# Attention stage cut into nine units instead of eleven, with fractional stage offsets, integer phases, and dense down products two parts behind

## The chip, the cores and the metric

The kernel runs on one core of a Trainium2 chip. The metric is the time of one execution on the device in microseconds (us). TensorE (PE in the profile) multiplies matrices, and its weight loads have a row of their own (PEld); VectorE is DVE, ScalarE is ACT, GpSimd is POOL, and SyncE (SP) issues most of the transfers.

## What is computed

Three layers in a row, in float32: a linear attention with a complex decay, a mixture of experts with one expert for each token, and a dense gated layer.

```python
# attention: batch 4, 8 heads, 768 tokens, head width 48
mag = np.sqrt(a_re * a_re + a_im * a_im)
scale = np.minimum(mag, 0.999) / (mag + 1e-06)
a_re_n, a_im_n = (a_re * scale, a_im * scale)
for t in range(S):
    ar, ai = (a_re_n[:, :, t, :, None], a_im_n[:, :, t, :, None])
    new_re = ar * S_re - ai * S_im
    new_im = ar * S_im + ai * S_re
    kv = np.einsum('bhd,bhe->bhde', k[:, :, t], v[:, :, t])
    S_re, S_im = (new_re + kv, new_im)
    y[:, :, t] = np.einsum('bhd,bhde->bhe', q[:, :, t], S_re)
# experts: 3072 tokens of width 384, 8 experts with 1024 hidden
logits = x @ w_gate + modality_bias[modality_id]
e_idx = np.argmax(logits, axis=1)             # gate_w: softmax value of that expert
out[mask] = gate_w[mask, None] * (np.maximum(x[mask] @ w1[e], 0.0) @ w2[e])
# dense: hidden 1536
g = x @ w_gate
silu = g * (1.0 / (1.0 + np.exp(-g)))
return (silu * (x @ w_val)) @ w_out
```

## The kernel before

**Attention.** The recurrence is worked in 24 chunks, one for each batch b and each stretch t of 128 tokens, all 8 heads at once. A chunk is a tile of 128 tokens by 384 (8 heads x 48). The decays become logarithms and angles. A product with a triangular matrix (`tri`) sums them along the tokens; the decay's sum is exponentiated into p and r = 1/p, the angle's sum is the phase, and sine and cosine of the phase stand in `tr`. k·r and q·p times `tr` give K and Q of 768 columns a chunk (L597). PE transposes them, multiplies them (L656), DVE masks the product with the triangle (`am`, L661), PE multiplies with v and adds the carried state (L670, L673), ACT copies the result (`yT`), and PE reorders it together with the router's logits (L684, "x of a chunk" below). L684 thus marks that a chunk of attention is done. The state (`S`) and the last phase (`carry`) go on to the chunk of the same batch at the next t.

**Units.** The elementwise stages are issued for a unit of up to three chunks, so an instruction has 384, 768 or 1152 columns. Before, `CUTS` makes eleven units of 1, 2, 3, 3, 3, 3, 3, 2, 2, 1 and 1 chunks. Chunks are counted c0 to c23 and units u0, u1, ... here. The stages of a unit are load_a (the decays a_re and a_im into `ar` and `ai`), a1 and a2 (logarithms, clamps), angle (arctangent), decay and sum (the two products with `tri` and what reads them), load_b (q, k, v), trig (sine and cosine), prod (k·r, q·p, K, Q), attend, and route (softmax, expert, position in the expert's region, rows written to DRAM by POOL).

**Who sets the order.** Each stage adds its operations to a planner (`Plan`, L24). The order in which they are added is the program's: `todo` sorts (u + lag, stage, u), with whole-number lags in `ROUND`. The planner (`order`, L79) then simulates the engines with cost estimates: at each step it emits the operation that can start earliest, a tie going to the one added first. `bias` adds a handicap to a choice of DVE and to a change of ACT's function table. Each engine runs its list strictly in the order emitted. Tiles come from rings of one to five buffers, so a new tile waits for the last reader of the old one.

**The phase before.** For each chunk ACT turns the phase in PSUM into a whole number of turns (`ki`, L533), DVE subtracts that many turns (`tw`, L538), and a clamp (L562) and an absolute value (L571, in place) run for each unit between and around the sine and the cosine.

**Experts.** The eight slots hold up to 396 rows each. The first slot's expert is guessed from the routing after unit uGU (before: GU = 5, 15 chunks), so its rows (`xg`) and weights (`st`) are fetched while attention still runs; first and second slot are planned with the attention stage. A slot is 8 hidden blocks of up products (L976), relu (`hh`, `hl`), down products (L990). Weights are split into two halves of bits: a cast (L1004, `w1h`, `w2h`) and a difference (L1006). Before the second slot's up products, every engine reads a flag `miss` (was the guess wrong?) and branches; before, that reading stands after the plan.

**Dense layer.** 8 blocks of 384 tokens and 12 parts of the hidden width: 96 rounds of 18 up products (pg, pv, L1517), the gate on ACT and DVE (L1520 to L1522, `hd` L1420 and L1421), and 9 down products (po, L1537: 3 groups t of 128 tokens, 3 products each). A round's down products follow the next round's up products. `write` (L1539) copies three groups (ACT, L1542) and POOL writes each to DRAM (L1544).

## Time and profile before

| | |
|---|---|
| median of 3 runs | 974.35 us (973.89 to 974.85) |
| the profiled execution's own time | 973.59 us |
| its span, first to last instruction | 971.8 us |
| mean granted TensorE clock | 0.984 of 2.4 GHz |
| PE, PEld busy | 913.3 us (94%), 868.8 us (89%) |
| DVE, ACT busy | 606.6 us (62%), 458.1 us (47%) |
| POOL busy | 115.6 us (12%) |
| bytes moved | 64.57 MB |

The profile times every instruction of one execution from the span's start. "Idle before" is the time that an engine stood still ahead of an instruction, and the arrow names what ended it. Attention fills about 0 to 280 us, the first slot 280 to 310 us, the other slots 311 to 501 us, and the dense layer what is left. The shares above are means over all of these.

### The profile page before, as it was taken

How to read it: one execution, taken by the hardware profiler on the slowest of the kernel's cores; microseconds unless marked ns; L12 is line 12 of the kernel's file. 1: busy time of each engine (PE TensorE's matmuls, PEld its weight loads, DVE VectorE, ACT ScalarE, POOL GpSimd, SP SyncE). 2: the span in 40 equal slices, each digit the busy share in tenths (PEclk: the TensorE clock that was granted, in tenths of full speed). 3: DMA queues.
4: the chain of work that ended last, by engine and by line, in shares of the span. 5: the costliest groups of instructions: out<-in, count | busy, mean ns of one | idle time of the engine just before them, and what ended most of it. 6: DMA issues, size and time to landing. Idle time of an engine off the chain costs nothing. (4 is left out here: it accounts for less than half of the span.)

```text
span 971.8 us, 15775 instructions
## 1 busy us (share of the span) xinstructions
PE 913.3 (94%) x5982; PEld 868.8 (89%) x5982; DVE 606.6 (62%) x1215; ACT 458.1 (47%) x798; POOL 115.6 (12%) x212
## 2 busy tenths in 40 slices
PE   2687999999988999999998899999999999999997
PEld 1466888988878999999997799999999999999996
DVE  6789989887775888788868843434333343433332
ACT  6787888786664555545444332322222232222222
POOL 2122022231220011111100010000101000010101
PEclk9887999999999999999999999999999999999999
DMA  9997365547422557333221000000000000000000
GB/s 170 161 183 142 74 132 101 101 100 206 117 65 75 95 97 215 78 78 88 55 67 49 1 25 1 1 25 1 25 1 26 1 9 17 1 25 1 25 1 25
DMA packets 155670, 64.57 MB, mean 66 GB/s; under 512 B 135564, under 2 KB 150212, under 8 KB 155588
## 3 DMA queue, kind: packets, MB, share of 16 engines
q1 hardware_dynamic: 147588, 39.82, 21.9%
q0 software_dynamic: 8000, 23.69, 9.2%
q8 instruction: 48, 0.79, 0.4%
q14 instruction: 34, 0.28, 0.1%
HBM read 67.86 MB, written 14.37 MB: 85 GB/s over the span
## 5 line engine op out<-in xcount | busy, mean ns | idle before, releaser
L1537 PE MATMUL po<-w,hd 128*128 128x384 f32 x864 | 168.9, 339 | 6.5 <-ACT hd L1420 6.4
L1517 PE MATMUL pg<-xb,w 128*128 128x384 f32 x864 | 166.1, 336 | 1.3 <-ACTq L1481 1.3
L1517 PE MATMUL pv<-xb,w 128*128 128x384 f32 x864 | 165.5, 336 | 0.0
L1537 PEld LDWEIGHTS po<-w,hd 128*128 128x128 f32 x864 | 150.4, 188 | 11.9 <-ACT hd L1420 9.1
L1521 DVE TENSOR_TENSOR sg<-sg,pg 128x384 f32<-128x384 f32 x96 | 53.2, 554 | 164.6 <-ACT sg L1520 164.6
L1517 PEld LDWEIGHTS pg<-xb,w 128*128 128x128 f32 x864 | 152.1, 188 | 1.6 <-ACTq L1481 1.6
L1517 PEld LDWEIGHTS pv<-xb,w 128*128 128x128 f32 x864 | 151.2, 188 | 0.0
L1420 ACT CAST hd<-sg 128x384 fp32r<-128x384 f32 x96 | 49.3, 513 | 161.3 <-DVE sg L1522 161.3
L1520 ACT ACTIVATE sg<-pg 128x384 f32<-128x384 f32 x96 | 47.2, 491 | 162.5 <-PE pg L1517 162.5
L1421 DVE TENSOR_TENSOR hd<-sg,hd 128x384 fp32r<-128x384 f32 x96 | 53.6, 558 | 55.6 <-ACT hd L1420 55.6
L1522 DVE TENSOR_TENSOR sg<-sg,pv 128x384 f32<-128x384 f32 x96 | 53.2, 554 | 37.3 <-PE pv L1517 36.3
L1544 POOL DMA_INDIRECT out_dram<-o,idu x24 | 23.1, 964 | 410.4 <-ACT o L1542 407.3
L976 PE MATMUL banks<-xh,w1h 128*128 128x396 f32 x192 | 67.0, 349 | 2.3 <-DVEq L1226 2.3
L979 ACT ACTIVATE hh<-banks 128x396 fp32r<-128x396 f32 x64 | 32.1, 502 | 76.0 <-PE banks L976 74.0
L976 PE MATMUL banks<-xh,w1l 128*128 128x396 f32 x192 | 66.2, 345 | 0.0
L983 DVE SCALAR_TENSOR_TENSOR hl<-banks,hh 128x396 fp32r<-128x396 f32 x64 | 36.3, 567 | 31.5 <-ACT hh L979 31.0
L656 PEld LDWEIGHTS banks<-tQ,tK 96*128 96x128 f32 x384 | 48.2, 196 | 5.2 <-issue 2.4
L656 PE MATMUL banks<-tQ,tK 96*128 96x128 f32 x384 | 52.2, 284 | 0.5 <-ACT tQ L380 0.4
L990 PE MATMUL banks<-hl,w2h 128*128 128x396 f32 x192 | 47.9, 344 | 1.2 <-DVE hl L983 1.2
L990 PE MATMUL banks<-hh,w2h 128*128 128x396 f32 x192 | 47.8, 343 | 0.3 <-ACT hh L979 0.3
L990 PE MATMUL banks<-hh,w2l 128*128 128x396 f32 x192 | 47.7, 343 | 0.0
L976 PE MATMUL banks<-xl,w1h 128*128 128x396 f32 x192 | 45.6, 346 | 0.0
(216 smaller groups left out, 1556.4 us busy)
## 6 DMA issues: line engine op xcount, KB each, us to landing
st<-in_moe_w_dram SPq DMA_DIRECT2D x64, 384.0 KB
xrows<-zero SPq DMA_DIRECT2D x8, 597.1 KB
xg<-xrows SPq DMA_DIRECT2D x8, 597.1 KB
ar<-in_a_re_dram SPq DMA_DIRECT2D x24, 192.0 KB
ai<-in_a_im_dram SPq DMA_DIRECT2D x24, 192.0 KB
q<-in_q_dram SPq DMA_DIRECT2D x24, 192.0 KB
k<-in_k_dram SPq DMA_DIRECT2D x24, 192.0 KB
v<-in_v_dram SPq DMA_DIRECT2D x24, 192.0 KB
```

What stands on the lines that cost most here:

```text
L656: pe.matmul(plan[ap][:, i * P : (i + 1) * P], plan[kt][:, i, :], plan[qt][:, i, :], start=True, stop=True)
L976: pe.matmul(ps[:, :SLOT], a[:, g, o : o + P], x[:, g, :], start=(n == 0), stop=(n == 3 * G3 - 1))
L979: sc.activation(out=hidden(s, f)[0], in_=ps[:, :SLOT], func=AF.Relu)
L983: ve.scalar_tensor_tensor(out=hl, in0=ps[:, :SLOT], scalar=0.0, in1=hh.bitcast(F32), op0=ALU.max, op1=ALU.subtract)
L990: pe.matmul(pds[:, g, :SLOT], w[:, f % 2, g * P : (g + 1) * P], x, start=(f == 0 and term == 0), stop=(f == KF1 - 1 and term == 2))
L1420: sc.copy(dst[0], src)
L1421: ve.tensor_tensor(out=dst[1], in0=src, in1=dst[0].bitcast(F32), op=ALU.subtract)
L1517: pe.matmul(p_, a[:, g, :], x[:, g, :n_], start=(n == 0), stop=(n == 3 * G3 - 1))
L1520: sc.activation(out=sg, in_=ps[0], func=AF.Sigmoid)
L1521: ve.tensor_tensor(out=sg, in0=sg, in1=ps[0], op=ALU.mult)
L1522: ve.tensor_tensor(out=sg, in0=sg, in1=ps[1], op=ALU.mult)
L1537: pe.matmul(p_[:, :DM], h[:, sl], w, start=(f == 0 and i == 0), stop=(f == KF2 - 1 and i == 2))
```

## The change

1. The attention stage has nine units: 2, 3, 3, 3, 3, 3, 2, 2 and 3 chunks.
2. Each stage's lag is a fraction of a round (`LAG`), scaled by 0.95 for the first two units, so the program's order and the planner's choices change throughout.
3. The phase: ACT writes the sum times 2^25/2π as an int32 straight into `tw`. For each unit DVE then shifts left by 7 (whole turns fall out of the word) and multiplies the int32 by π/2^31 into float32. L538 and L562 go, with the tile `ki`. The absolute value goes to a tile `ta` of its own; `jk` (a discarded output) goes to `w`. The carried phase is taken after the multiplication.
4. The guess of the first expert comes after u3 (11 chunks) instead of u5 (15 chunks).
5. Reading the flag `miss` becomes an operation inside the plan.
6. The planner's bias numbers and the estimate for the constants' load change.
7. In the dense layer a round's down products come two rounds later; at the end, the last two parts run group by group, each group written as soon as it is done.

```diff
-    CUTS = (1, 2, 3, 3, 3, 3, 3, 2, 2, 1, 1)
+    CUTS = (2, 3, 3, 3, 3, 3, 2, 2, 3)
...
+    SHL = 7
+    TURN = 2.0 ** (32 - SHL)
+    RAD = 3.1415925 / 2.0**31
...
+            def f_tw(e, c=c, pk=pk):
+
+                if e == "ACT":
+                    sc.activation(out=plan[tw][:, c, :].bitcast(I32), in_=plan[pk][:, :DM], func=AF.Copy, scale=TURN / TWO_PI)
...
+        def f_shl():
+
+            ve.tensor_scalar(out=flat(tw).bitcast(I32), in0=flat(tw).bitcast(I32), scalar1=SHL, scalar2=None,
+                             op0=ALU.logical_shift_left)
+
+        def f_rad():
+            ve.tensor_scalar(out=flat(tw), in0=flat(tw).bitcast(I32), scalar1=RAD, scalar2=None, op0=ALU.mult)
...
-            def f_tw(c=c, pk=pk, kk=kk):
-                ve.scalar_tensor_tensor(out=plan[tw][:, c, :], in0=plan[kk], scalar=-TWO_PI, in1=plan[pk][:, :DM],
-                                        op0=ALU.mult, op1=ALU.add)
...
-        def f_cl():
-            ve.tensor_scalar(out=flat(tw), in0=flat(tw), scalar1=3.1415925, scalar2=-3.1415925, op0=ALU.min, op1=ALU.max)
...
-    exv, g_row, GU = {}, [], 5
+    exv, g_row, GU = {}, [], 3
...
-    ROUND = (("load_a", 0), ("angle", 1), ("trig", 2), ("a1", 0), ("load_b", 1), ("a2", 0), ("decay", 1),
-             ("prod", 2), ("sum", 1), ("attend", 2), ("route", 3))
-    todo = sorted((u + lag, i, u, nm) for i, (nm, lag) in enumerate(ROUND) for u in range(NU))
+    LAG = dict(load_a=0.00, angle=1.30, trig=2.25, a1=1.00, load_b=2.35, a2=1.00, decay=1.45, prod=2.45, sum=1.65, attend=2.90, route=4.55)
+    todo = sorted((u + lag * (1 if u >= 2 else 0.95), i, u, nm) for i, (nm, lag) in enumerate(LAG.items()) for u in range(NU))
...
-    plan.emit(rank=lambda o, p: o["i"], delta=0, bias={'DVE': 2.0, 'table': 0.6}, pins={'sx': 'ACT', 'abs': 'DVE', 'ki': 'ACT'})
+    missing = []
+    plan.op("SP", 0.0, lambda: missing.append(nc.values_load(miss32[0:1, 0:1], min_val=0, max_val=1000001)), r=["miss"])
+    plan.emit(rank=lambda o, p: o["i"], delta=0.00, bias={'DVE': 1.41, 'table': 0.37}, pins={'sx': 'ACT', 'abs': 'DVE', 'ki': 'ACT'})
...
-    miss = nc.values_load(miss32[0:1, 0:1], min_val=0, max_val=1000001)
-    missed = tc.If(miss > 0, label="missed")
+    missed = tc.If(missing[0] > 0, label="missed")
...
-        if n > 0:
-            jp, fp = seq[n - 1]
+
+        if 1 < n < len(seq) - 1:
+            jp, fp = seq[n - 2]
             down2(jp, fp)
             if fp == KF2 - 1:
                 write(jp)
-    down2(*seq[-1])
-    write(len(BLKS) - 1)
+
+    down2(*seq[-3])
+    for t in range(BLK // P):
+        for jp, fp in seq[-2:]:
+            down2(jp, fp, (t,))
+        write(len(BLKS) - 1, (t,))
```

Line numbers of the changed kernel differ: x of a chunk is L696 there, first-slot up and down products L988 and L1002, the split's cast L1016, the dense products L1529 and L1550.

**SP at the start of the program, before.** Each row is a run of transfers of one chunk each (128x8x48) into the ring buffers of `ar`, `ai`, q, k and v; a unit's `ar` and `ai` come first, and its q, k and v later.

```order
L403 DMA ar_157<-in_a_re_dram 128x8x48
L403 DMA ai_160<-in_a_im_dram 128x8x48
L403 DMA ar_158<-in_a_re_dram 128x8x48 x2
L403 DMA ai_161<-in_a_im_dram 128x8x48 x2
L403 DMA q_168<-in_q_dram 128x8x48
L403 DMA k_170<-in_k_dram 128x8x48
L403 DMA v_172<-in_v_dram 128x8x48
L403 DMA ar_159<-in_a_re_dram 128x8x48 x3
L403 DMA ai_162<-in_a_im_dram 128x8x48 x3
L403 DMA q_169<-in_q_dram 128x8x48 x2
```

The same stretch of SP in the changed kernel:

```order
L407 DMA ar_157<-in_a_re_dram 128x8x48 x2
L407 DMA ai_160<-in_a_im_dram 128x8x48 x2
L407 DMA ar_158<-in_a_re_dram 128x8x48 x3
L407 DMA ai_161<-in_a_im_dram 128x8x48 x3
L407 DMA ar_159<-in_a_re_dram 128x8x48 x3
L407 DMA ai_162<-in_a_im_dram 128x8x48 x3
L407 DMA q_168<-in_q_dram 128x8x48 x2
L407 DMA k_170<-in_k_dram 128x8x48 x2
L509 DMA pe_206<-p_174 16x1x48 x2
L407 DMA v_172<-in_v_dram 128x8x48 x2
```

The decays of three units (8 chunks, 16 transfers) now stand ahead of the first q and k; before, three chunks' decays (6 transfers) did.

**ACT at the end of the first slot, before.** `hh` are relu rows of the first slot, `w1h` and `w2h` casts of the second slot's weights from the staging tiles `st_0` to `st_3`, `xg` the scaling of the second slot's rows, `xh` the cast of these rows once PE has transposed them, and the TENSOR_LOAD reads the flag.

```order
L875 ACTIVATE xg_2537<-xg_2537 99x384
L1004 CAST w2h_2547<-st_3_128 128x768
L979 ACTIVATE hh_2551<-banks 128x396
L1004 CAST w1h_2542<-st_0_121 128x768
L979 ACTIVATE hh_2550<-banks 128x396
L1004 CAST w2h_2546<-st_0_125 128x768
L979 ACTIVATE hh_2551<-banks 128x396
L1004 CAST w1h_2543<-st_1_122 128x768
L1018 CAST xh_2539<-banks 128x396 x3
L1004 CAST w2h_2547<-st_1_126 128x768
L1132 TENSOR_LOAD miss_137
L1226 COMPARE_AND_BRANCH
```

The same stretch of ACT in the changed kernel:

```order
L991 ACTIVATE hh_2290<-banks 128x396
L991 ACTIVATE hh_2291<-banks 128x396
L1016 CAST w1h_2282<-st_0_121 128x768
L1137 TENSOR_LOAD miss_137
L1016 CAST w2h_2286<-st_0_125 128x768
L1016 CAST w1h_2283<-st_1_122 128x768
L1016 CAST w2h_2287<-st_1_126 128x768
L887 ACTIVATE xg_2277<-xg_2277 99x384 x4
L1030 CAST xh_2279<-banks 128x396 x3
L1238 COMPARE_AND_BRANCH
```

The scaling of `xg` and the cast of `xh` moved behind the last `hh` and behind all weight casts, where before they stood between them; the flag's read moved ahead of the last three weight casts.

**DVE where the fifth chunk (c4) gets its K and Q, before.** The K and Q rows (L597) are those of c3 and then c4, both of unit u2; `ai`, `sx`, `ar` and `w` belong to the preparation (a1, a2) of later units, `S` is the state, `tw` the phase.

```order
L597 TENSOR_TENSOR K_1_194<-k_170,tr_177 128x768
L597 TENSOR_TENSOR Q_1_196<-q_168,tr_177 128x768
L597 TENSOR_TENSOR K_0_193<-k_170,tr_177 128x768
L597 TENSOR_TENSOR Q_0_195<-q_168,tr_177 128x768
L457 TENSOR_TENSOR ai_160<-ai_160,ar_158 128x1152
L460 TENSOR_SCALAR ai_160<-ai_160 128x1152
L464 SCALAR_TENSOR_TENSOR sx_165<-sx_165,w_167 128x1152
L621 TENSOR_TENSOR S_200<-banks,pt_206 96x8x48
L597 TENSOR_TENSOR K_1_194<-k_170,tr_177 128x768
L597 TENSOR_TENSOR Q_1_196<-q_168,tr_177 128x768
L538 SCALAR_TENSOR_TENSOR tw_176<-ki_179,banks 128x384
```

The same place in the changed kernel, where c4 is the last chunk of u1; `k_170` and `q_168` are those of the next unit, u2:

```order
L600 TENSOR_TENSOR k_170<-k_170,r_175 128x1152
L600 TENSOR_TENSOR q_168<-q_168,p_174 128x1152
L609 TENSOR_TENSOR K_0_191<-k_171,tr_178 128x768
L609 TENSOR_TENSOR Q_0_193<-q_169,tr_178 128x768
L548 TENSOR_SCALAR tw_176<-tw_176 128x1152
L552 TENSOR_SCALAR tw_176<-tw_176 128x1152
L673 TENSOR_TENSOR am_189<-banks,tri 128x512
L673 TENSOR_TENSOR am_190<-banks,tri 128x512
L633 TENSOR_TENSOR S_198<-banks,pt_205 96x8x48
L462 TENSOR_TENSOR ai_163<-ai_163,ar_157 128x1152
L515 COPY pt_204<-banks 96x24
L465 TENSOR_SCALAR ai_163<-ai_163 128x1152
```

Counted from the first decay of unit u0, 99 rows stand ahead of c4's K before, and 66 now. Ahead of c4's K now stand k·r and q·p of u2 (L600), which need the transfers of u2's k and q.

## Rows read from the trace of the kernel before

**Rows 1.** Busy time of the engines in three stretches: window, its length, busy (count), clock, DMA.

```profile
0.00:100.00 100.00, 65.67 (x411) 49.39 (x412) 82.06 (x148) 76.42 (x109) 19.88 (x54) 0.88 1.03 159
100.00:240.00 140.00, 139.13 (x1391) 122.96 (x1390) 121.84 (x259) 111.33 (x186) 31.84 (x51) 1.00 0.56 122
240.00:280.00 40.00, 35.18 (x354) 30.69 (x354) 30.27 (x100) 31.29 (x59) 11.18 (x19) 1.00 0.36 102
```

**Rows 2.** Waits of PE, 0 to 100 us: total, times, longest.

```profile
PE banks L489 <- DVE sx L464: 16.5, 3, 10.4
PE banks L643 <- ACT r L492: 4.5, 2, 2.7
```

**Rows 3.** Waits of PE, 100 to 240 us (both that there are).

```profile
PE banks L529 <- DVE tw L538: 0.6, 1, 0.6
PE banks L643 <- ACT tK L380: 0.3, 1, 0.3
```

**Rows 4.** Timeline of PE: start, busy, engine and line; x of c4, then of c23.

```profile
104.58 1.10 PE L684 MATMUL banks<-pick_g,yT 128*128 128x104 f32 x8
...
276.94 1.06 PE L684 MATMUL banks<-pick_g,yT 128*128 128x104 f32 x8
280.07 0.17 PE L769 MATMUL banks<-o,tris 128*128 128x8 bf16 x1 [2.06 <-DVE o L758]
```

**Rows 5.** Timeline of DVE from the start, 0 to 36 us.

```profile
5.48 0.56 DVE L422 SCALAR_TENSOR_TENSOR ar<-ar 128x384 f32<-128x384 f32 x1
...
15.75 1.36 DVE L422 SCALAR_TENSOR_TENSOR ar<-ar 128x1152 f32<-128x1152 f32 x1 [3.59 <-DMA ar<-in_a_re_dram]
...
26.51 0.96 DVE L597 TENSOR_TENSOR K<-k,tr 128x768 f32<-128x768 f32 x1 [0.68 <-ACT tr L575]
27.38 0.95 DVE L597 TENSOR_TENSOR Q<-q,tr 128x768 f32<-128x768 f32 x1
...
31.48 1.36 DVE L422 SCALAR_TENSOR_TENSOR ar<-ar 128x1152 f32<-128x1152 f32 x1 [3.08 <-DMA ar<-in_a_re_dram]
```

**Rows 6.** DVE by line and shape, 100 to 240 us: busy, mean ns, idle.

```profile
L661 DVE TENSOR_TENSOR am<-banks,tri 128x512 f32<-128x512 f32 x30 | 20.3, 684 | 4.4 <-PE banks L656 3.8
...
L538 DVE SCALAR_TENSOR_TENSOR tw<-ki,banks 128x384 f32<-128x384 int32 x13 | 6.9, 549 | 0.2 <-ACT ki L533 0.2
...
L562 DVE TENSOR_SCALAR tw<-tw 128x1152 f32<-128x1152 f32 x3 | 2.2, 749 | 0.0
```

**Rows 7.** Timeline of PE and ACT where the second slot takes over, 290 to 312 us.

```profile
292.18 0.45 PE L990 MATMUL banks<-hl,w2h 128*128 128x396 f32 x1 [1.18 <-DVE hl L983]
...
293.96 0.62 ACT L875 ACTIVATE xg<-xg 99x384 f32<-99x384 f32 x1 [2.53 <-DMA xg<-xrows]
...
306.48 1.18 PE L995 MATMUL banks<-ident,xg 99*128 99x99 f32 x12
307.02 1.27 ACT L1018 CAST xh<-banks 128x396 fp32r<-128x396 f32 x3 [0.73 <-PE banks L995]
...
308.98 0.34 PE L990 MATMUL banks<-hl,w2h 128*128 128x396 f32 x1
309.35 0.83 ACT L1004 CAST w2h<-st 128x768 fp32r<-128x768 f32 x1 [1.06 <-PE banks L990]
...
311.63 0.42 PE L976 MATMUL banks<-xh,w1h 128*128 128x396 f32 x1 [2.31 <-DVEq L1226]
```

**Rows 8.** Timeline of DVE and PE near the dense layer's start, 548 to 559 us.

```profile
552.60 0.56 DVE L1421 TENSOR_TENSOR hd<-sg,hd 128x384 fp32r<-128x384 f32 x1 [0.58 <-ACT hd L1420]
...
552.62 2.08 PE L1537 MATMUL po<-w,hd 128*128 128x384 f32 x9 [1.61 <-ACT hd L1420]
```

**Rows 9.** Timeline of the last writes, 959 to 972 us.

```profile
961.47 3.43 PE L1537 MATMUL po<-w,hd 128*128 128x384 f32 x18
963.90 1.52 ACT L1542 COPY o<-po 128x384 f32<-128x384 f32 x3 [1.12 <-PE po L1537]
...
967.18 0.96 POOL L1544 DMA_INDIRECT out_dram<-o,idu  x1 [0.19 <-issue]
```

More of the change, by code (lines that the diff above doesn't have):

```diff
@@ L424, in f_bad @@
         def f_bad():
[L425 removed]
+            ve.scalar_tensor_tensor(out=flat(w), in0=flat(sq), scalar=X_MIN, in1=flat(sx), op0=ALU.subtract,
                                     op1=ALU.is_lt, accum_out=cnt[:, u : u + 1])
@@ L439, in stage_a1 @@
         plan.op("DVE", t_dve(W), f_sq, w=sqs)
-        plan.op("DVE", t_dve(W), f_bad, r=sqs + [sx], w=[jk, ("cnt", u)], new=[("jk", jk)])
+        plan.op("DVE", t_dve(W), f_bad, r=sqs + [sx], w=[w, ("cnt", u)], new=[("w", w)])
         plan.op("DVE", t_dve(W), f_sum, r=sqs, w=[sx])
@@ L467, in stage_a2 @@
         plan.op("ACT", t_act(W), f_ri, w=ris + ["ACT"], table=LOGEXP)
-        plan.op("ACT", t_act(W), f_w, r=[sx], w=[w, "ACT"], new=[("w", w)], table=LOGEXP)
+        plan.op("ACT", t_act(W), f_w, r=[sx], w=[w, "ACT"], table=LOGEXP)
         plan.op("DVE", t_dve(W), f_rt, r=ris, w=ais)
@@ L544, in stage_sum @@
-            plan.op({"DVE": t_dve(DM), "ACT": t_act(DM)}, 0, f_ki, r=[pk], w=[kk], kind="ki")
-            plan.op("DVE", t_dve(DM), f_tw, r=[pk, kk], w=[tc_])
+            plan.op("PE", 0.65, f_mm, r=[lc], w=[pk], new=[("B", pk)] + ([("tw", tw)] if c == 0 else []))
+            plan.op({"DVE": t_dve(DM), "ACT": t_act(DM)}, 0, f_tw, r=[pk], w=[tc_], kind="ki")
+        def f_shl():
+            ve.tensor_scalar(out=flat(tw).bitcast(I32), in0=flat(tw).bitcast(I32), scalar1=SHL, scalar2=None,
+                             op0=ALU.logical_shift_left)
@@ L546, in stage_sum, with f_carry @@
+        def f_rad():
+            ve.tensor_scalar(out=flat(tw), in0=flat(tw).bitcast(I32), scalar1=RAD, scalar2=None, op0=ALU.mult)
+        W = len(units[u]) * DM
+        plan.op("DVE", t_dve(W, True), f_shl, w=each("tw", u))
+        plan.op("DVE", t_dve(W, True), f_rad, w=each("tw", u))
+        for c, (b, t) in enumerate(units[u]):
+            def f_carry(c=c, b=b):
+                gp.dma_start(carry[b], plan[tw][P - 1 : P, c, :])
             if t < NC_ - 1:
-                plan.op("Pool", 1.0, f_carry, r=[tc_], w=[ck], lat=3.0)
+                plan.op("Pool", 1.0, f_carry, r=[tw + (c,)], w=[("carry", b)], lat=3.0)
@@ L556, in part, with angles @@
             return plan[tr].rearrange("p c h r d -> p (c h) r d")[:, : n * H, i, :]
[L558 to L562 removed]
+        def angles(key):
+            return flat(key).rearrange("p (a d) -> p a d", d=D)
         def f_sn():
[L565 removed]
+            sc.activation(out=part(1), in_=angles(tw), func=AF.Sin)
         def f_abs(e):
             if e == "ACT":
[L569 removed]
+                sc.activation(out=flat(ta), in_=flat(tw), func=AF.Abs)
             else:
[L571 removed]
+                ve.tensor_scalar(out=flat(ta).bitcast(I32), in0=flat(tw).bitcast(I32), scalar1=0x7FFFFFFF, scalar2=None,
                                  op0=ALU.bitwise_and)
         def f_cs():
[L575 to L577 removed]
+            sc.activation(out=part(0), in_=angles(ta), func=AF.Sin, scale=-1.0, bias=halfpi)
         plan.op("ACT", t_act(W), f_sn, r=tws, w=[tr + (1,), "ACT"], new=[("tr", tr)], table=TRIG)
[L579 to L580 removed]
+        plan.op({"DVE": t_dve(W, True), "ACT": t_act(W)}, 0, f_abs, r=tws, w=[ta], new=[("ta", ta)], kind="abs")
+        plan.op("ACT", t_act(W), f_cs, r=[ta], w=[tr + (0,), "ACT"], table=TRIG)
     def stage_prod(u):
@@ L1116, in tile_kernel @@
     plan.op("DVE", 0.5, flag_2, r=["sum"], w=["bad"])
-    gone = [k for u in range(NU) for nm in EARLY for k in [(nm, u)] + each(nm, u)] + [("ki", *bt) for bt in order]
+    gone = [k for u in range(NU) for nm in EARLY for k in [(nm, u)] + each(nm, u)]
     plan.op("SP", 0.0, make_room, w=["room"], past=gone)
@@ L1527, in tile_kernel, with down2 @@
     po = {}
-    def down2(j, f):
-        hh, hl = hd.pop((j, f))
+    def down2(j, f, ts=range(BLK // P)):
+        hh, hl = hd[j, f]
         oh_, ol_ = wd[f][2]
@@ L1533, in down2 @@
             po[j] = [dp_o.tile([P, BLK], F32, name=f"po{t}") for t in range(BLKS[j][1] // P)]
-        for t, p_ in enumerate(po[j]):
+        for t in ts:
+            p_ = po[j][t]
             sl = slice(t * P, (t + 1) * P)
@@ L1537, in down2, with write @@
                 pe.matmul(p_[:, :DM], h[:, sl], w, start=(f == 0 and i == 0), stop=(f == KF2 - 1 and i == 2))
-    def write(j):
-        for t, p_ in enumerate(po[j]):
+    def write(j, ts=range(BLK // P)):
+        for t in ts:
+            p_ = po[j][t]
             o = dfou.tile([P, DM], F32, name="o")
```

30 lines of the change are left out of this document (8 added, 22 removed).

## The prediction

> **What bounds the kernel now.** I read three stretches of attention side by side first: busy time of each engine in 0 to 100, 100 to 240 and 240 to 280 us [rows 1]. PE is busy 65.67 of the first 100 us, 139.13 of the next 140, and 35.18 of the last 40. The waits of PE say the same: in the first stretch 16.5 us go to three waits for the decay's logarithm (L464), 4.5 to `r` and 2.6 to K [rows 2]; in the second there are two waits, 0.9 us together [rows 3]. So the middle follows PE, and the ramp follows what feeds it, mostly DVE (82.06 of 100 us).
>
> The timeline of PE gives the pace. The x of the fifth chunk, c4, starts at 104.58 us and that of the last, c23, at 276.94 [rows 4]: 19 chunks in 172.36 us, 9.07 each. Up to 104.58 there are only five chunks, 20.9 us each. What the ramp loses against the middle's pace is thus large, and no other place in the program has as much idle PE. Behind c23 PE stands 2.06 us for the last router's result. The first slot has a stall of 1.18 us and the second begins 2.65 us after the first one's last down product started [rows 7].
>
> **The ramp.** DVE is in order, so I add up what its list in the changed kernel holds until c4's last mask, starting with the first decay at 5.48 us [rows 5]. Consecutive operations of DVE start closer together than the length of one: K of 768 columns is 0.96 us long, and the Q behind it starts 0.87 later, so I take 0.09 off every length. Counts are from the changed list, prices from [rows 5] and [rows 6]:
> - 17 two-source operations of 768 columns at 0.87: 14.8
> - 23 of 1152 at 1.27 (1.36 less 0.09): 29.2
> - 9 one-source ones of 1152 at 0.66 (L562, 0.749), and 4 of 768 at some 0.48 by width: 7.9
> - 10 masks at 0.60 (0.684): 6.0
> - 6 state updates of 384 columns, two sources as L538 has (0.549), at 0.46: 2.8
> - small ones: an estimate of 5
>
> That is 65.7 us. To it come the start, 5.48, about 2 for results that the next operation reads, and waits for transfers. Today's list waits 3.59 and 3.08 us for `ar` [rows 5]; in the new one 16 decay transfers stand ahead of the first q, so I allow 10.5 in all. The sum is 83.7. The x follows its last mask by about 3 us on PE, so c4's x comes near 87 us, 17.6 earlier than 104.58. I take 15.0 of this, since PE waits between c0 and c4 are sure to add something. Why it is shorter: before, 99 rows of DVE stood ahead of c4's K, now 66; the ones left out are the preparation of later units, which today runs about 3.5 chunks further ahead at this point.
>
> **The middle.** PE has the same products, so 9.07 us a chunk stays. But DVE now does that preparation later. In 100 to 240 us it is busy 121.84 of 140, 87% [rows 1]; some 14 us of deferred work go into about 176 us. Against that stand savings: L538, 24 times 0.549 less 0.09 is 11.0, and the clamp L562 about 5 more; added are a shift and a multiplication for each unit, both one-source like L562 if they run at its rate (11 us in all; 16 if the int32 multiplication goes at 1.27 a 1152, which no row shows; I take the first, since source and result have four bytes as L562's have). Two rounds of router less on DVE are 4 to 5 us. Net saving some 8 to 9 us, so DVE stands near 90%. I charge 2.0 us of new PE waits.
>
> Weighed against this, the Trainium skill (Perfetto Trace Analysis, section Identifying the Most-Contended Engine) says that matmul busy time is no measure of how near TensorE is to its limit, and weight-load busy time is. Weight loads are busy 122.96 of 140 us here, 88% [rows 1], so by that page PE would have room in the middle, and the sum would end near 952 (the second rival) instead of 961. The waits [rows 3] don't show that room: an engine with 12% to spare should be seen waiting, and PE waits 0.9 of 140 us.
>
> **The end of attention and the two slots.** The last router stands behind the first slot's first up products now, so the 2.06 us wait ahead of them [rows 4] goes: −2.1. The last unit has three chunks instead of one, with less behind it to fill: an estimate of +2.0, about one wait like that. The 1.18 us stall and a smaller one of 0.29 in the first slot come from a weight that arrives late; its transfers now stand ahead of the last units' loads in SP's list: −1.5.
>
> At the handover, ACT's list puts the four scalings of `xg` and the three casts `xh` behind the last weight cast, and that cast waits for the last down product. Before, it began at 309.35, 0.37 after that product's start, and lasted 0.83 [rows 7]. From the product's start the new chain is: 0.37, the cast 0.83, the scalings 4 times 0.54 (0.62 less overlap) 2.15, rest of the transposes 0.4, casts 1.27, the difference 0.55 and the branch 0.45, the branch taken from the distance of today's last difference to PE's first product. With some 0.4 for the flag's read on ACT that is 6.4 us instead of 2.65. The 12 transposes leave the time before (about 1 us). +3.0. Ahead of the first relu, ACT also copies rows whose buffer waits for the last unit but two: +1.0.
>
> **The dense layer.** In the first rounds DVE also splits weights, and the down products wait for `hd`: PE starts a round's down at 552.62 after 1.61 idle, once ACT has the first half of `hd`, while DVE only begins the second [rows 8]. Two rounds late, they have their `hd` long before; but the splits stay, so part of the wait can turn up elsewhere. I count this one wait less 0.6 that returns: −1.0. In the steady state PE has no wait to lose. At the end the first copy starts at 963.90, 2.4 us after the first of the last 18 down products [rows 9]; the writes follow at 1.27 us each, so the end follows the first copy. With six products to a group, of which three are ready early, the first copy comes at 962.6 or before: −1.3.
>
> **Sum.** −15.0 + 2.0 − 2.1 + 2.0 − 1.5 + 3.0 + 1.0 − 1.0 − 1.3 = −12.9. Against the profiled execution's own 973.59 that is 960.7. The median of before is 0.76 above that execution, so 961.5; I say 961.
>
> **Rivals.**
> 1. *The gain is given back in the middle.* The 14 us of preparation that the ramp leaves out cost DVE time later. If DVE at 87% has no room for it, PE waits, and 12 of the 15 us return: 973. For it: DVE's share. Against it: DVE has 18 us idle in the middle's 140, and its list gets lighter. Chance 0.12.
> 2. *PE has room.* Weight loads are busy 122.96 of 140 us in the middle [rows 1]. If the rest is room that matmuls lend and take back, the middle follows DVE and ACT in part, and the net 8 to 9 us of DVE savings count too: 952. Against it: 0.9 us of waits in 140 [rows 3]. Chance 0.12. This is the case for which the page of the Trainium skill named above speaks.
> 3. *Slower: the transfers.* c4's K stands behind k·r and q·p of u2 on DVE, and the last piece of u2's k is the 49th load, with a fill of `xrows` as large as three loads ahead. DVE would come there at about 57 us. Today the 24th load has landed by 31.48 [rows 5], 1.31 us a load; at 159 GB/s in the whole stretch [rows 1], a load of 0.197 MB is 1.24. At 1.14, which an emptier queue could reach, k is there at 59 or 60; at 1.31, at 68, and the time is about 970. From about 1.45 the delay eats all of the 12.9; at 1.5 the kernel is slower, 976. For it: DMA share 1.03 in the stretch. Against it: the waits of DVE on transfers are 6.7 us today. Chance of the middle case 0.10, of slower 0.08.
> 4. *The change to phases and lags does nothing*, and only the ends and the dense layer remain: 2.0 − 2.1 − 1.5 + 4.0 − 2.3 is 0.1, so 974. Chance 0.05.
>
> **Numbers.** The forecast, a gain of 9 to 18, has 0.53. Its own range is 956 to 966. Low end of the whole: rival 2 with a full ramp, 949; high end: rivals 1 and 4, 973. About 0.2% (2 us) is what a measurement of this kernel tells from no change. Faster by more: the forecast, rival 2, the middle case of 3, and most of 1: 0.84. Within: 0.07. Slower: 0.09.
>
> **What would show it.** In the changed profile: x of c4 (L696) near 87 us, first x later than 42; 9.1 us a chunk after; first slot's first up product (L988) near 266; no wait for a weight in the first slot; about 6 us between its last down product and the next up product; no wait for `hd` in the dense layer's first rounds; first copy of the tail 1.3 us or more ahead of the last. Wrong it would be if DVE waits for q or k beyond 15 us in the ramp, or if waits of PE for masks or K pass 10 us in the middle.

## The result and the profile after

The changed kernel takes 950.21 us (median of 4 runs, 949.85 to 950.48) against 974.29 of the kernel before: a ratio of 0.9748, with a 95% interval of 0.9736 to 0.9760. Its profiled execution took 950.28 us with a span of 948.6. The time lies in the predicted range of 949 to 973, but below the forecast's own range of 956 to 966: the gain is 24 us where 13 were forecast.

Busy time of the engines in the three stretches of [rows 1]:

```profile
0.00:100.00 100.00, 73.38 (x557) 58.73 (x557) 85.44 (x138) 84.04 (x120) 18.46 (x52) 0.91 1.13 176
100.00:240.00 140.00, 140.00 (x1409) 124.29 (x1409) 125.38 (x265) 115.46 (x190) 43.30 (x59) 1.00 0.61 132
240.00:280.00 40.00, 40.00 (x318) 38.20 (x318) 24.59 (x78) 17.39 (x34) 8.05 (x15) 1.00 0.13 44
```

Between 100 and 280 us PE is busy without a break. Before, it lost 0.87 us up to 240 and 4.82 in the 40 us behind. From x of c4 to the first up product PE is busy for 169.8 us in both kernels; before, it also stood still for 5.76 us there. All the waits of PE that are left in attention stand in the ramp, for the decay's logarithm and for one K:

```profile
PE banks L494 <- DVE sx L469: 23.7, 2, 16.6
PE banks L626 <- DVE K L609: 2.6, 1, 2.6
PE banks L696 <- ACT yT L384: 0.3, 1, 0.3
```

x of c4, of the last two chunks together, and the first up product of the first slot, on PE's timeline (against [rows 4]):

```profile
86.86 1.04 PE L696 MATMUL banks<-pick_g,yT 128*128 128x104 f32 x8
...
254.83 2.03 PE L696 MATMUL banks<-pick_g,yT 128*128 128x104 f32 x16
256.63 0.43 PE L988 MATMUL banks<-xh,w1h 128*128 128x396 f32 x1
```

On DVE's timeline, k·r of u2 behind its transfer, and c4's last mask:

```profile
62.53 1.36 DVE L600 TENSOR_TENSOR k<-k,r 128x1152 f32<-128x1152 f32 x1 [1.12 <-DMA k<-in_k_dram]
...
82.27 0.68 DVE L673 TENSOR_TENSOR am<-banks,tri 128x512 f32<-128x512 f32 x1
```

From these starts the gain can be laid out by stretches, in spans (971.8 to 948.6, −23.2). Where several products stand in one row its start counts. The cut at c4 is the prediction's. The gain is not the same at its neighbours: x of c3 is 18.8 us earlier (95.79 to 77.01), x of c5 13.8 (112.77 to 98.98), since the new units end at other chunks.

| stretch | before | after | difference | predicted |
|---|---|---|---|---|
| start to x of c4 | 104.58 | 86.86 | −17.7 | −15.0 |
| x of c4 to first up product | 175.54 | 169.77 | −5.8 | +1.9 |
| first slot, to second slot's first product | 31.51 | 31.93 | +0.4 | +2.5 |
| second slot's first product to dense layer's first | 191.36 | 192.44 | +1.1 | 0 |
| dense layer and writes | 468.81 | 467.60 | −1.2 | −2.3 |

The handover to the second slot on PE and ACT (against [rows 7]): last down product, last weight cast, the four scalings of `xg`, the cast `xh`, and the first products.

```profile
282.67 0.34 PE L1002 MATMUL banks<-hl,w2h 128*128 128x396 f32 x1
...
283.04 0.83 ACT L1016 CAST w2h<-st 128x768 fp32r<-128x768 f32 x1 [0.54 <-PE banks L1002]
283.78 2.13 ACT L887 ACTIVATE xg<-xg 99x384 f32<-99x384 f32 x4
286.31 1.27 ACT L1030 CAST xh<-banks 128x396 fp32r<-128x396 f32 x3 [0.40 <-PE banks L1007]
...
288.56 0.67 PE L988 MATMUL banks<-xh,w1h 128*128 128x396 f32 x1 [1.61 <-DVEq L1238]
289.02 0.53 PE L988 MATMUL banks<-xh,w1l 128*128 128x396 f32 x1
```

From the last down product's start to the next up product it is 5.89 us, where 6.4 were worked out and 2.65 stood before. The cost shows twice: the product behind the longer pause starts at half clock. The granted clock of the first 10 us of the second slot is 0.66 after (first row) and 0.83 before (second row, of the kernel before), with 37 and 44 products:

```profile
288.00:298.00 10.00, 9.44 (x37) 9.47 (x38) 6.88 (x19) 3.50 (x5) 0.00 (x0) 0.66 0.23 64
```

```profile
311.00:321.00 10.00, 9.37 (x44) 9.39 (x44) 6.63 (x19) 4.58 (x7) 0.00 (x0) 0.83 0.22 62
```

In the dense layer, the waits of the up products for the gate's first step (`sg`), which stands before them now:

```profile
PE pg L1529 <- DVE sg L1533: 6.1, 6, 1.9
```

That is 6.1 us in 6 waits, where the down products waited 6.4 us in 7 for `hd`; [rows 8] shows one of those. Of the dense layer, the table's −1.2 compares executions at different clocks: over the layer's first 70 us the granted clock was 1.00 before and 0.95 in this one. From the first up product of the dense layer to the end, the new one took 467.6 to 467.7 us in four kernels at 0.95 (this and three below) and 466.1 to 466.3 in four at 1.00; the old one took 470.2 at 0.95 and 468.8 at 1.00. At like clocks it is thus 2.5 us shorter. The tail (against [rows 9]): the last 27 down products, the first copy, the last write.

```profile
937.80 4.85 PE L1550 MATMUL po<-w,hd 128*128 128x384 f32 x27
...
940.60 0.48 ACT L1556 COPY o<-po 128x384 f32<-128x384 f32 x1 [1.50 <-PE po L1550]
...
943.89 0.97 POOL L1558 DMA_INDIRECT out_dram<-o,idu  x1 [0.19 <-issue]
```

The first copy starts 2.80 us after the first of the 27, and two more groups follow while POOL writes; counted from the last up products (pv at 936.24, before at 959.91), less one round of down products of 1.56 us that was put off to there, the end comes 1.1 us sooner.

### The profile page after: what moved, and what is told of

The parts are those of the page before. It is cut to its first block, busy times and chain, and to the rows that moved or that the text cites. A ratio compares the mean times of both kernels' runs of the same rounds, so it can differ in the third digit from the quotient of the medians.

```text
span 948.6 us, 15710 instructions
## 1 busy us (share of the span) xinstructions
PE 904.9 (95%) x5980; PEld 868.9 (92%) x5980; DVE 594.7 (63%) x1147; ACT 448.9 (47%) x775; POOL 120.6 (13%) x210
## 5 line engine op out<-in xcount | busy, mean ns | idle before, releaser
L1529 PE MATMUL pg<-xb,w 128*128 128x384 f32 x864 | 167.6, 338 | 7.4 <-DVE sg L1533 6.1
L1529 PE MATMUL pv<-xb,w 128*128 128x384 f32 x864 | 167.6, 339 | 0.0
L1550 PE MATMUL po<-w,hd 128*128 128x384 f32 x864 | 165.7, 337 | 0.0
L1529 PEld LDWEIGHTS pg<-xb,w 128*128 128x128 f32 x864 | 152.2, 188 | 9.7 <-DVE sg L1533 8.1
L1529 PEld LDWEIGHTS pv<-xb,w 128*128 128x128 f32 x864 | 153.5, 191 | 0.0
L1550 PEld LDWEIGHTS po<-w,hd 128*128 128x128 f32 x864 | 151.6, 188 | 0.0
L988 PE MATMUL banks<-xh,w1h 128*128 128x396 f32 x192 | 67.6, 352 | 1.6 <-DVEq L1238 1.6
L988 PE MATMUL banks<-xh,w1l 128*128 128x396 f32 x192 | 66.8, 348 | 0.0
L1002 PE MATMUL banks<-hh,w2l 128*128 128x396 f32 x192 | 47.7, 343 | 0.0
L1002 PE MATMUL banks<-hh,w2h 128*128 128x396 f32 x192 | 47.7, 343 | 0.0
L1002 PE MATMUL banks<-hl,w2h 128*128 128x396 f32 x192 | 47.7, 343 | 0.0
L988 PE MATMUL banks<-xl,w1h 128*128 128x396 f32 x192 | 45.9, 348 | 0.0
```

The source lines that it names most:

```text
L988: pe.matmul(ps[:, :SLOT], a[:, g, o : o + P], x[:, g, :], start=(n == 0), stop=(n == 3 * G3 - 1))
L1002: pe.matmul(pds[:, g, :SLOT], w[:, f % 2, g * P : (g + 1) * P], x, start=(f == 0 and term == 0), stop=(f == KF1 - 1 and term == 2))
L1529: pe.matmul(p_, a[:, g, :], x[:, g, :n_], start=(n == 0), stop=(n == 3 * G3 - 1))
L1550: pe.matmul(p_[:, :DM], h[:, sl], w, start=(f == 0 and i == 0), stop=(f == KF2 - 1 and i == 2))
```

## The experiments

Each was compared with the kernel before on its own chip, where that ran at 974.75 or 975.05 us. The changed kernel's 950.21 us come from the run above, so a difference from it rests on the ratios to the kernel before. The executions of one kernel lie 1 to 9 us apart there, so small differences are read from the stretches of the trace. Each trace is one execution, though, and starts scatter too: the run with the old dense layer has the changed kernel's attention, and its x of c4 came at 88.11 us and its first up product at 257.89, both 1.3 later. With the old lags the scatter is larger (below).

**Old units.** The changed kernel with the eleven units.

```diff
-    CUTS = (2, 3, 3, 3, 3, 3, 2, 2, 3)
+    CUTS = (1, 2, 3, 3, 3, 3, 3, 2, 2, 1, 1)
-    exv, g_row, GU = {}, [], 3
+    exv, g_row, GU = {}, [], 4
```

> The changed kernel with the eleven old units (1, 2, 3, 3, 3, 3, 3, 2, 2, 1, 1), the guess after u4 (12 chunks); lags, phases and dense layer stay new. Theory (the first two units hold five chunks, so c4's K needs only two units' preparation ahead of it): c4's K falls back from 66 rows behind the first decay to 86, some 14 us later, so x of c4 near 100 us, and the two small last units bring back 3 us or more of waits at the end of attention: about 966 us. Rival (the fractional lags do it): c4 near 88 us and about 953 us.

958.67 us, ratio 0.9823 [0.9796, 0.9849]. x of c4 came at 91.29 us, 4.4 later than in the changed kernel and not 13; the first up product at 268.12, 11.5 later. The router's wait of 2.1 us at the end of attention is back. So the units are worth 8 us in this company, more than half of it behind c4. Neither forecast was met: counting the rows ahead of c4's K foretold its time badly.

**Old lags.** The changed kernel with `ROUND`, the old bias and the old estimate for the constants.

```diff
-    LAG = dict(load_a=0.00, angle=1.30, trig=2.25, ...)
+    ROUND = (("load_a", 0), ("angle", 1), ("trig", 2), ...)
-    bias={'DVE': 1.41, 'table': 0.37}
+    bias={'DVE': 2.0, 'table': 0.6}
```

> The changed kernel with the old whole-number lags, the old planner bias and the old estimate for the constants' load; units, phases and dense layer stay new. Theory (units): c4's K stands 58 rows behind the first decay instead of 66, so x of c4 is at 80 to 88 us, and the time is 950 us, 4 either way. Rival (lags): x of c4 falls back to 98 us or later, and the time to 962 us or more.

964.38 us, ratio 0.9887 [0.9863, 0.9910]; x of c4 at 100.48. My theory fell: c4's K stands earlier in DVE's list than in the changed kernel, and its x came 13.6 us later. The first up product came at 271.00, 14.4 later, so nearly all of the loss is there at c4. The trace shows a slow stretch ahead of it. Two waits of PE, then the granted clock of 70 to 88 us (third column from the end), then x of c4:

```profile
69.83 0.64 PE L655 MATMUL banks<-ident,K 128*96 128x128 f32 x4 [0.65 <-DVE S L633]
71.63 1.09 PE L655 MATMUL banks<-ident,Q 128*96 128x128 f32 x4 [1.16 <-ACT r L497]
...
70.00:88.00 18.00, 16.84 (x89) 15.15 (x87) 15.65 (x28) 14.66 (x24) 2.36 (x3) 0.53 1.18 167
...
100.48 1.03 PE L696 MATMUL banks<-pick_g,yT 128*128 128x104 f32 x8
```

Behind 1.8 us of waits PE worked at half clock to 88 us, in a stretch with much to do (16.84 of 18 us busy).

**Old lags, with PE kept busy.**

```diff
+                        if (u, c, hf) == (1, 1, 0):
+                            warm(plan[pk], dict(tK=3, tQ=5)[nm])   # 128x128 products on constants
```

> The changed kernel with the old whole-number lags and bias, as in the run a_lag_old, and 8 more matmuls of 128x128 on constants, overwritten unread, where PE waits 0.65 and 1.16 us ahead of transposes of c3; all else in the same order. In that run the clock was 0.50 from 71.6 to 88 us behind these waits, and x of c4 was at 100.48. Theory (the slow clock is what put c4 back): the clock stays near 1.00 from 66 to 88, x of c4 comes 5 to 8 us earlier, and the time falls from 964.4 to 957 to 960. Rival (c4 is late for DVE's sake): x of c4 within 2 us of 100.5, and 963 to 965.

The clock from 66 to 84 us (18 us again, 4 earlier), a wait of PE for a mask, and x of c4:

```profile
66.00:84.00 18.00, 14.84 (x111) 13.01 (x110) 16.37 (x29) 14.06 (x24) 2.36 (x3) 0.81 1.15 188
...
75.36 0.97 PE L689 MATMUL banks<-am,v 128*64 128x128 f32 x8 [2.32 <-DVE am L680]
...
95.64 1.03 PE L703 MATMUL banks<-pick_g,yT 128*128 128x104 f32 x8
```

x of c4 came 4.84 us earlier and the first up product 4.9 (266.11 for 271.00). But most of this was there before the first added product, which starts at 65.38 us. Up to that place every engine has the same list in both kernels, and x of c0 already came at 51.64 instead of 56.09. The clock from 36 to 54 us and x of c0, first without the added products, then with them:

```profile
36.00:54.00 18.00, 14.66 (x83) 12.44 (x81) 14.60 (x22) 11.88 (x20) 3.38 (x7) 0.62 0.92 158
...
56.09 1.14 PE L696 MATMUL banks<-pick_g,yT 128*128 128x104 f32 x8
```

```profile
36.00:54.00 18.00, 15.04 (x121) 12.81 (x122) 16.44 (x27) 15.59 (x26) 4.26 (x6) 0.91 0.90 161
...
51.64 1.14 PE L703 MATMUL banks<-pick_g,yT 128*128 128x104 f32 x8
```

So two executions of the same lists differ by 4.45 us at c0, at a clock of 0.62 and 0.91 ahead of it. From c0 to c4 it is 44.39 us without the added products and 44.00 with them: they are worth 0.4 us. They put PE 2.9 us further ahead by 80 us, and it lost most of that to the wait of 2.32 us for the mask, which is also why the clock is 0.81 and not 1.00. The median is 962.43 us (ratio 0.9882 [0.9862, 0.9902]), no change against the run without the products (0.9887). So it is not shown that the half clock from 70 to 88 us put c4 back. Some 4.4 of the 13.6 us may belong to the one execution that was read there; why the old lags cost the rest stays open.

**Old phases.** The changed kernel with L538, the clamp and the absolute value in place.

```diff
+            def f_tw(c=c, pk=pk, kk=kk):
+                ve.scalar_tensor_tensor(out=plan[tw][:, c, :], in0=plan[kk], scalar=-TWO_PI, in1=plan[pk][:, :DM],
+                                        op0=ALU.mult, op1=ALU.add)
...
-        plan.op("DVE", t_dve(W, True), f_shl, w=each("tw", u))
-        plan.op("DVE", t_dve(W, True), f_rad, w=each("tw", u))
```

> The changed kernel with the old phase (whole turns subtracted for each chunk, clamp, absolute value in place); units, lags and dense layer stay new. Theory (the middle follows PE, so lighter phases on DVE pay only in the ramp): for 8 chunks the old form costs DVE some 2 us more up to c4, so c4's x near 89 us and about 952.5 us, with no new PE waits in the middle. Rival (the middle follows DVE as well): the whole net saving of 8 us returns, 958 us or more, with PE waits in the middle of 5 us or more.

970.65 us, ratio 0.9957 [0.9937, 0.9977]: with the old phases, the new units, lags and dense layer are worth 4 us of the 24. Neither theory had this: the price of 20 us is three times the DVE time that the phases save (25.5 us of operations on `tw` here, 18.6 on `tw` and `ta` in the changed kernel). x of c4 is at 100.32, the first up product at 280.62. Between the two PE stands still for 8.05 us, where the rival asked for 5 or more; in the changed kernel it does not stand still there at all. On ACT, the sine of u0, a square that waits for a transfer, and the cosine:

```profile
28.84 0.84 ACT L570 ACTIVATE tr<-tw 128x768 f32<-128x768 f32 x1 [0.46 <-DVE tw L567]
33.23 1.16 ACT L388 ACTIVATE sx<-ai 128x1152 f32<-128x1152 f32 x1 [3.55 <-DMA ai<-in_a_im_dram]
34.30 0.92 ACT L580 ACTIVATE tr<-tw,halfpi 128x768 f32<-128x768 f32 x1
```

and the same two rows of the changed kernel, with nothing between them:

```profile
28.47 0.84 ACT L578 ACTIVATE tr<-tw 128x768 f32<-128x768 f32 x1
29.22 0.92 ACT L588 ACTIVATE tr<-ta,halfpi 128x768 f32<-128x768 f32 x1
```

The cosine reads what the absolute value wrote over the sine's input, so the planner put the square into the gap, and the square waited 3.55 us.

**New units alone**, on the kernel before.

```diff
-    CUTS = (1, 2, 3, 3, 3, 3, 3, 2, 2, 1, 1)
+    CUTS = (2, 3, 3, 3, 3, 3, 2, 2, 3)
-    exv, g_row, GU = {}, [], 5
+    exv, g_row, GU = {}, [], 4
```

> The kernel before with the nine new units alone, the guess after u4 (14 chunks; before 15); whole-number lags, old phases and old dense layer stay. Theory (units): c4's K stands 75 rows behind the first decay instead of 99, so c4's x near 89 us instead of 104.6, and the waits at the end of attention (4.8 us) mostly go: about 956 us. Rival (lags): 968 us or more.

1083.7 us, ratio 1.1113 [1.1088, 1.1138]. But in the slots PE ran 264 products of each kind here where it ran 192 before, that is eleven slots instead of eight, which took 112 us longer from the first up product to the dense layer, and the output is wrong. Why is not known, so the time as a whole says nothing about the units, and only attention is read, with that caution. x of c4 came at 95.18 and the first up product at 276.65, 3.5 us before that of the kernel before. Most of the 9.4 us gained at c4 were given back by the end.

**PE kept busy in the changed kernel.**

```diff
+                if u == 1 and not warmed:
+                    warmed.append(1)
+                    warm(plan[pk], 27)
...
+                if (u, c) == (1, 0):
+                    warm(plan[dk], 10)
```

> The changed kernel with 37 more matmuls of 128x128 on constants, whose results are overwritten unread: 27 ahead of the decay sum of u1, where PE waits 7.14 us from 21.9 us on, and 10 ahead of the first K product of c2, where it waits 2.58 us from 54.2 on. All other operations keep their order on every engine. Behind these waits the granted clock is 0.50 to 36 us and from 56 to 63. Theory (after a wait PE works at half clock, and that is part of the ramp's price): the clock stays near 1.00, PE is 3 to 6 us ahead afterwards where it is late, x of c4 comes 1 to 4 us earlier, and the time is 947 to 949. Rival (in the ramp only DVE counts): x of c4 unchanged or later, 950 to 951.

Two stretches of the changed kernel, then the same of this one with its x of c4:

```profile
20.00:36.00 16.00, 8.86 (x20) 4.22 (x18) 14.15 (x18) 15.44 (x23) 2.06 (x3) 0.68 1.34 179
52.00:64.00 12.00, 9.15 (x43) 6.86 (x43) 10.29 (x23) 10.98 (x18) 2.36 (x3) 0.72 1.39 182
```

```profile
20.00:36.00 16.00, 13.50 (x86) 10.34 (x85) 14.17 (x18) 15.94 (x23) 2.06 (x3) 1.00 1.35 181
52.00:64.00 12.00, 10.91 (x70) 7.33 (x69) 11.65 (x25) 11.97 (x18) 2.36 (x3) 1.00 1.18 179
...
87.42 0.81 PE L706 MATMUL banks<-pick_g,yT 128*128 128x104 f32 x6
```

The clock went from 0.68 and 0.72 to 1.00, and x of c4 came 0.6 us later: 950.48 us, ratio 0.9739 [0.9723, 0.9756], no change. Here the rival is right. The trace shows where the clock's gain went: the last of four phase products started at 32.08 us instead of 35.38, and PE then waited 1.36 us for a carried phase (at 35.46) and 1.80 for a mask (at 43.97).

**More work on DVE, same order.**

```diff
+                    ve.scalar_tensor_tensor(out=extra, in0=extra, scalar=0.5, in1=extra, op0=ALU.mult, op1=ALU.mult)
```

> The changed kernel with one operation more on DVE for each chunk, of the old L538's size (two sources, 384 columns, 0.55 us) on a tile that nothing else reads, at the place where the chunk's phase is converted; all else in the same order. DVE has 24 times 0.46, 11 us, more to do, more than the new phases saved. Theory (what the new phases save in DVE time is worth something in the ramp only): x of c4 at 90 to 92, PE waits in the middle under 2 us, 953 to 955 us. Rival (DVE's load explains the 20 us between this kernel and the run with the old phases): 962 us or more.

The added operations by line (24, 548 ns each), and x of c4:

```profile
L539 DVE SCALAR_TENSOR_TENSOR extra<-extra 128x384 f32<-128x384 f32 x24 | 13.1, 548 | 0.1
...
86.77 1.04 PE L699 MATMUL banks<-pick_g,yT 128*128 128x104 f32 x8
```

950.54 us, ratio 0.9757 [0.9741, 0.9773]. Eight of the added operations, 3.7 us, stand ahead of c4's x, and it did not come later; the first up product came 1.5 us later, at 258.09. DVE took the work up in its waits: from its first decay to c4's last mask they are 6.9 us here and 10.4 in the changed kernel. So 11 us of DVE time are worth some 1.5 us in this order, hardly more than the 1.3 by which two executions of one attention differ, and by this the 6.9 us that the phases save would be worth no more. DVE's load does not explain the 20.

**Old bias numbers.**

```diff
-    bias={'DVE': 1.41, 'table': 0.37}
+    bias={'DVE': 2.0, 'table': 0.6}
```

> The changed kernel with the planner's two bias numbers of before (2.0 and 0.6 instead of 1.41 and 0.37), which decide which of two engines copies a tile and when ACT changes its function table; units, lags, phases and guess stay new. Theory (the gain hangs on one particular interleaving, in which PE hardly waits): x of c4 or the waits at the end move by several us, 955 to 965 us. Rival (units, lags and phases carry the gain): 950 to 952 us.

947.93 us, ratio 0.9724 [0.9708, 0.9740]: 2.3 us under the changed kernel, though the two intervals overlap. The theory fell; the gain does not hang on these numbers. x of c4 is at 86.55, the first up product at 258.81, 2.2 later. The handover is the better for it. Last down product, all transposes at once, first up product:

```profile
284.60 0.35 PE L1002 MATMUL banks<-hl,w2h 128*128 128x396 f32 x1
284.79 1.25 PE L1007 MATMUL banks<-ident,xg 99*128 99x99 f32 x12
288.45 0.65 PE L988 MATMUL banks<-xh,w1h 128*128 128x396 f32 x1 [2.40 <-DVEq L1238]
```

3.85 us instead of 5.89, as the scalings of `xg` again stand ahead of the first slot's end. So the second slot begins at the same time (288.45 and 288.56), and behind the shorter pause the clock of the next 10 us is 0.83 instead of 0.66: from there to the dense layer it takes 191.21 us instead of 192.44. The rest of the 2 us is the clock in the dense layer, 1.00 here and 0.95 in the changed kernel's execution, which the run with more work on DVE has too and which is not this edit's.

**Absolute value in place**, all else as in the changed kernel.

```diff
-        plan.op({"DVE": t_dve(W, True), "ACT": t_act(W)}, 0, f_abs, r=tws, w=[ta], new=[("ta", ta)], kind="abs")
-        plan.op("ACT", t_act(W), f_cs, r=[ta], w=[tr + (0,), "ACT"], table=TRIG)
+        plan.op({"DVE": t_dve(W, True), "ACT": t_act(W)}, 0, f_abs, w=tws, kind="abs")
+        plan.op("ACT", t_act(W), f_cs, r=tws, w=[tr + (0,), "ACT"], table=TRIG)
```

> The changed kernel with one thing back: the absolute value of the phase overwrites the phase instead of going to a tile of its own, so it has to wait for the sine, and the cosine for it; integer phases, units, lags and bias stay new, and DVE has the same work. In the run with the old phases ACT began the sine of u0 at 28.84 and the cosine at 34.30, having taken up work in between that waited 3.55 us for a transfer; in the changed kernel the two stand 0.75 us apart. Theory (the chain sine, absolute value, cosine through one tile is what the 20 us of the old phases hang on): x of c4 at 93 us or later, and 958 to 970 us. Rival (the chunk's own subtraction and its PSUM bank, or the conversion, are the cause): x of c4 within 2 us of 86.9, and 949 to 953 us.

961.45 us, ratio 0.9864 [0.9839, 0.9889], 11 us more with the same instructions. The price is right and the place is not: x of c4 came at 84.74, but the next only at 106.16, where the changed kernel has it at 98.98, and the first up product at 265.42, 8.8 later. ACT there: the cosine of a unit, and the phase conversions of the next; between them, a phase product on PE.

```profile
84.00 1.26 ACT L588 ACTIVATE tr<-tw,halfpi 128x1152 f32<-128x1152 f32 x1
...
92.41 0.49 ACT L536 ACTIVATE tw<-banks 128x384 int32<-128x384 f32 x1 [0.24 <-PE banks L531]
...
94.28 0.98 PE L531 MATMUL banks<-ai,tri 128*128 128x384 f32 x1 [1.91 <-DMA ai<-carry]
...
95.93 0.49 ACT L536 ACTIVATE tw<-banks 128x384 int32<-128x384 f32 x1 [2.57 <-PE banks L531]
```

In the changed kernel:

```profile
79.81 1.27 ACT L588 ACTIVATE tr<-ta,halfpi 128x1152 f32<-128x1152 f32 x1
...
88.65 0.49 ACT L536 ACTIVATE tw<-banks 128x384 int32<-128x384 f32 x1
...
90.18 0.86 ACT L536 ACTIVATE tw<-banks 128x384 int32<-128x384 f32 x2
```

There the cosine reads `ta`; it begins 4.2 us sooner, and the conversions begin 3.8 us sooner and end 7.4 sooner. But the rows do not show a conversion waiting for the one buffer of `tw`: the cosine had ended 7 us before the first of them, and the wait of 2.57 us is for phase products, of which one waited 1.91 us for the carried phase. The edit also acts through the planner, which orders every engine's list by what each operation waits for. The 11 us are the price of the dependence and of the new order together; no run changed the tile and kept the order.

**New phases alone**, on the kernel before. The edit is that of the change (integer turns, `f_shl`, `f_rad`, the tile `ta`, `jk` to `w`).

> The kernel before with the new phases alone (integer turns, absolute value in a tile of its own, the discarded output to the tile w); units, lags, bias, guess and dense layer stay old. Theory (the phases shorten the chain to K by themselves): x of c4 at 92 to 98 us instead of 104.6, the first up product at 266 to 272 instead of 280.1, and 960 to 966 us. Rival (phases pay only together with the new units and lags): the first up product at 277 or later, and 970 us or more.

x of c4 and the first up product:

```profile
90.13 1.04 PE L696 MATMUL banks<-pick_g,yT 128*128 128x104 f32 x8
...
266.73 0.42 PE L988 MATMUL banks<-xh,w1h 128*128 128x396 f32 x1
```

960.67 us, ratio 0.9845 [0.9818, 0.9871]: the phases alone bring 14 us, 14.5 of them at c4 and 13.4 at the first up product. The theory is right; c4 came even earlier than its 92 to 98 us.

**Old dense layer.** The edit takes the change's last diff lines back.

> The changed kernel with the old dense layer: down products one round behind, the last part over all groups before the writes. Theory (the waits at the dense layer's start only changed their place, from the down products to the up products, and only the tail gained): 951.2 us, about 1.0 more, with 6 us of PE waits for the gate's result again. Rival (the prediction's terms for start and tail, 2.3): 952.5.

952.71 us, ratio 0.9762 [0.9743, 0.9781], 2.5 more than the changed kernel, though the two intervals overlap. From the first up product of the dense layer to the end it is 470.2 us at a clock of 0.98, where the new one took 467.6 at 0.95: the rival, that is the prediction's own terms, is right. The down products wait 6.3 us for `hd` again, as much as the up products do in the new order, but a round of down products behind a wait took 2.08 us before [rows 8], 0.35 more than one without, and a round of up products behind one takes 1.83 to 1.85, 0.1 more (one round at half clock aside, 2.58 us). My theory had left that out.

**Old phases and old bias numbers.** Both edits above.

> The changed kernel with the old phases and the planner's old bias numbers (2.0, 0.6). With the new phases these numbers gave 2 us less than the new ones. Theory (the old phases are slow in whatever order): 964 us or more. Rival (the run with the old phases and the new bias fell on an unlucky order): below 960 us.

971.79 us, ratio 0.9971 [0.9948, 0.9995]. With the bias that is no worse for the new phases, the old ones stay as slow, as the theory had it. x of c4 is at 94.80 and the first up product at 276.03, 7.9 and 19.4 us later than in the changed kernel: the place of c4 does not foretell that of the end.

## Why the prediction was right in its sign and off in its size

**The ramp (−15.0, measured −17.7).** The sum over DVE's list gave the last mask at 83.7 us; it ended at 82.95, and x of c4 came at 86.86 for the 87 worked out. The 2.6 us that were held back for PE's waits were not needed. Up to the end of that mask DVE's list held 80.2 us of work and 15.8 of waits before, and 67.1 and 10.4 after. That the total fits so well is partly luck: 12.5 us of waits were put in, 10.5 of them for transfers, transfers took 3.0 and the results of ACT and PE 6.0, while the work was 67.1 us and not 65.7. And the sum is no bound: with 3.7 us more work in the same list c4 came at the same time, as the waits shrank from 10.4 to 6.9 us. The step that failed is "DVE is in order, so I add up": it priced the new order, and not what an edit to it is worth. It also gave the credit to the order of the preparation; the phases alone move c4 by 14.5 us, units alone by 9.4.

**The middle and the end (+1.9, measured −5.8).** This is the largest error. The pace of 9.07 us a chunk was taken from c4 to c23 and called PE's; it held the waits at the end of attention, 4.8 us, and 0.9 before. PE's busy time over this stretch is the same in both kernels, 169.8 us, and its waits are 5.76 us before and none after: that is the whole −5.8. So the step that failed is "9.07 us a chunk stays", with the 2.0 for new waits in the middle and the 2.0 for draining a unit of three: no wait came, and those there were went. Of the 5.76 us, 2.06 are the last router, which no longer stands ahead of the up products; what filled the rest was not tested.

**The phases.** Costed as DVE time, net 8 to 9 us together with two rounds of router. The terms as written add up to 9 or 10, of which the phases have 5; by the lengths in the traces the phases save 6.9 us. Either is beside the point, as 11 us more on DVE cost 1.5. What the prediction had at nothing is the tile: the absolute value in a tile of its own is alone worth 11 us, by its dependences and by the order that the planner makes of them; which link of these costs the time is not shown. By subtraction the other 9 of the 20 would lie in the chunk's own subtraction, its `ki` buffers, the PSUM bank held until then, or the carried phase; no run told these apart.

**The slots (+2.5, measured +0.4, and +1.1 behind).** The handover was worked out at 6.4 us and took 5.89. The copy ahead of the first relu, priced at 1.0, cost nothing that is seen: the first slot has no wait but those at its end. The half clock behind the longer pause was not in the sum.

**The dense layer (−2.3, measured −1.2 in these two executions and −2.5 at like clocks).** Right in size: the tail gave −1.1 for −1.3. At the start, in the run with the old bias, whose clock there is 1.00 as before, it is 453.95 us from the first to the last up products, or 455.51 with the round of down products put off, against 456.92: −1.4 for −1.0. But it came in another way than the term had it: the wait moved whole from the down products to the up products, and what was gained is that the round behind a wait is 0.1 us longer instead of 0.35.

**The rivals.** The first (973) did not come: PE waits for nothing from 100 to 280 us. The second gave 952, which is near the result by luck, as its mechanism is not borne out: PE has no room in that stretch, and 11 us of DVE time are worth 1.5 us in the new order. The rule behind it (the Trainium skill, Perfetto Trace Analysis, Identifying the Most-Contended Engine) takes weight-load busy time as the measure of how near TensorE is to its limit. The trace of after goes against it: weight loads are busy 124.29 of 140 us, 89%, while PE is busy throughout and waits for nothing. The third (transfers) did not come: k of u2 held DVE up by 1.12 us at 62.53, which is 1.2 us a load. The fourth, that phases and lags do nothing, is refuted by both: each is worth some 14 us or more.

## What to carry to other kernels

An engine's list with its waits added up gave the time of this order, but not the price of an edit: before pricing an operation by its length, ask what reads and writes its tile, and for how long its buffer is held. An operation in place between two readers ties all three into one chain, and here a second tile was worth more than all the DVE time saved. A trace is one execution: before a difference between two traces is put down to an edit, find where it begins. If it begins ahead of the edited place, the edit did not make it. A pace taken from two distant rows holds every wait between them, so the waits at the end of a stage belong in a window of their own.

## What the runs showed that was not expected

- The parts do not add up. Phases alone bring 14 us, and all the other parts without the phases 4; together they bring 24. Taking one part away costs 8 (units), 14 (lags and bias) or 20 us (phases).
- Keeping PE busy over its waits raised the clock from 0.90 to 0.98 (20 to 105 us) in the changed kernel and gained nothing, and gained 0.4 us up to c4 with the old lags. Yet two executions of the same lists differed by 4.45 us at c0, at a clock of 0.62 and 0.91 ahead of it, and kept that difference to the first up product.
- The two bias numbers of before are no worse for the new kernel than those that came with it: 947.93 us, with a handover of 3.85 us; some 1.2 us of the gain can be placed.
- The clock granted in the dense layer's first 70 us took one of a few values (0.95, 0.98, 1.00) in kernels with the same code there. The time of the layer was 1.4 us longer at 0.95 than at 1.00; at 0.98 it was 467.5 us in one kernel and 466.2 in another.
